# Loading attention values in 2 KB rows and rearranging them through DRAM, and loading the last 64 tokens of q and k in 1 KB rows

## The chip, the cores and the metric

The kernel runs on one core of one Trainium2 chip. The metric is the device time of that core in microseconds (us). "Fast" and "slow" are states of an execution; verdicts use fast runs alone. TensorE is PE in the profile, its weight loads PEld, VectorE DVE, ScalarE ACT, GpSimd POOL, and SyncE SP; a q behind a name (SPq, ACTq) is the engine's sequencer, which waits and issues transfers.

## The reference

```python
# q, k, v: (8, 8, 576, 64) float32
scores = scale * np.matmul(q, k.transpose(0, 1, 3, 2))
mask_local = (rel >= 0) & (rel < 32)                     # heads 0 to 3
mask_strided = (rel >= 0) & (pos_k % 32 == pos_q % 32)   # heads 4 to 7
attn = softmax(np.where(masks, scores, -1e9))
x = np.matmul(attn, v)            # -> (4608, 512), heads side by side
h = ((x @ w1) * (x @ w2)) @ w3
out = h @ w_out                   # (4608, 512) float32
```

## The kernel before

The weights w3 and w_out are first multiplied into one matrix (the "fold"). The attention of the 8 batches runs interleaved with that fold and with the dense matmuls: while the dense part of batch b runs, PE does the attention of batch b + 1 in between, in a program order that is fixed. Loads for batch b + 2 are issued a turn ahead by SP, go through nine staging buffers and are cast to fp16 by POOL.

The local heads work on 6 blocks of 96 queries, and each block reads 128 keys and values, 32 of them from the block before. So the value tile `v16L` holds token 96·t + p − 32 on partition p for block t, and its first 32 partitions repeat what other partitions hold. Before, each head is loaded with one 256-byte row per token, POOL casts it, and DVE copies the 32 repeated tokens:

```python
def load_vL(b):
    vt = v16L[b % 2]
    for hp in range(2):
        hs = slice(2 * hp, 2 * hp + 2)
        st = stgp.tile([P, 2, LT, D], FP32, tag="stg")
        for h in range(2):
            nc.sync.dma_start(st[32:P, h], v[b, 2 * hp + h].rearrange("(t p) d -> p t d", p=LQ))
        for pr in (bass.ds(32, 32), bass.ds(64, 64)):
            nc.gpsimd.tensor_copy(out=vt[pr, hs, :, 0:D], in_=st[pr])
        nc.vector.tensor_copy(out=vt[0:32, hs, 1:LT, 0:D], in_=vt[96:P, hs, 0:LT - 1, 0:D])
```

The last 64 tokens of q and k (`load_rest`) also come in 256-byte rows, in two transfers per batch. `ph_R` transposes them on PE and four copies put them behind the first 512 tokens:

```python
def ph_R(b):
    ...
    for i, (eng, t) in enumerate((("a", qT), ("a" if b < AHEAD else "v", kT))):
        copy(eng, t[:, 0:2, c0:c0 + NR], pv[:, 0:2, i])                    # contiguous write
        copy(eng, t[:, 2:4, 0:S]...[:, :, :, 64:SQ], pv[:, 2:4, i]...)
```

The order of use, for batch b and its first pair of heads (`...` are cuts):

```python
add(ph_S, pairs[p])        # scores: sps, then exp (ACT: pte) and mask (DVE: ptm)
...
add(ph_PV, pairs[p], 0)    # first local product: xps <- ptm, v16L
```

The softmax here doesn't subtract the row's maximum and nothing guards it: scores larger than these inputs give would overflow.

Of the kernel before, what the change touches and what calls it, by code (L numbers as in the profile page):

```python
# [8 lines left out]
FP32 = mybir.dt.float32  # L9
FP16 = mybir.dt.float16  # L10
# [4 lines left out]
def _ap(t: bass.AP, off_add, dims):  # L15
    return bass.AP(tensor=t.tensor, offset=t.offset + off_add, ap=dims)
# [3 lines left out]
def kernel(  # L20
# [11 lines left out]
    nc = tc.nc  # L32
    B, H, S, D = q.shape
# [3 lines left out]
    P = 128  # L37
# [10 lines left out]
    LQ, LT = 96, 6  # L48
    SQ, ST = 72, 8
    NM = 512  # L50
    NR = S - NM
    KW = 640

    consts = ctx.enter_context(tc.tile_pool(name="consts", bufs=1))
    stgp = ctx.enter_context(tc.tile_pool(name="stgp", bufs=9))
    qkp = ctx.enter_context(tc.tile_pool(name="qkp", bufs=2))
    att = ctx.enter_context(tc.tile_pool(name="att", bufs=2))
    ffn = ctx.enter_context(tc.tile_pool(name="ffn", bufs=2))
    psF = ctx.enter_context(tc.tile_pool(name="psF", bufs=3, space=bass.MemoryType.PSUM))
    psB = ctx.enter_context(tc.tile_pool(name="psB", bufs=2, space=bass.MemoryType.PSUM))  # L60
    psM = ctx.enter_context(tc.tile_pool(name="psM", bufs=1, space=bass.MemoryType.PSUM))
# [3 lines left out]
    def pe(ins):  # L65
        return tc.keep_in_program_order(ins)

    def copy(eng, out, in_):
        if eng == "a":
            nc.scalar.copy(out=out, in_=in_)  # L70
        elif eng == "v":
            nc.vector.tensor_copy(out=out, in_=in_)  # L72
        else:
            nc.gpsimd.tensor_copy(out=out, in_=in_)  # L74


    id16 = consts.tile([P, P], FP16)
# [24 lines left out]
    nc.vector.tensor_mul(maskS, mps[0:SQ, 0:SQ], causal)  # L102


    v16L = [consts.tile([P, 4, LT, D + 1], FP16, name=f"v16L{i}") for i in range(2)]
    v16S = [consts.tile([SQ, 4, ST, D + 1], FP16, name=f"v16S{i}") for i in range(2)]


# [2 lines left out]
    ptms = [consts.tile([P, 640], FP16, name=f"ptm{i}") for i in range(4)]  # L111
    nc.vector.memset(kT[:, 0:2, 0:32], 0.0)
    nc.vector.memset(kT[:, 2:4, S:KW], 0.0)
    for i in range(2):
        nc.vector.memset(v16L[i][:, :, :, D], 1.0)
        nc.vector.memset(v16L[i][0:32, :, 0, :], 0.0)
        nc.vector.memset(v16S[i][:, :, :, D], 1.0)
    for i in range(4):
        nc.vector.memset(ptms[i][:, 576:640], 0.0)
# [43 lines left out]
            x16[(b, nm, grp)] = t  # L163

    def load_rest(b, eng="p"):
        st = stgp.tile([P, H, D], FP32, tag="stg")
        for i, ten in enumerate((q, k)):
            nc.sync.dma_start(st[64 * i:64 * i + 64], ten[b, :, NM:S].rearrange("h p d -> p h d"))
        t = qkp.tile([P, H, D], FP16, tag="r")
        copy(eng, t, st)  # L170
        x16[(b, "r")] = t

    def load_vL(b):
        vt = v16L[b % 2]
        for hp in range(2):
            hs = slice(2 * hp, 2 * hp + 2)
            st = stgp.tile([P, 2, LT, D], FP32, tag="stg")
            for h in range(2):
                nc.sync.dma_start(st[32:P, h], v[b, 2 * hp + h].rearrange("(t p) d -> p t d", p=LQ))
            for pr in (bass.ds(32, 32), bass.ds(64, 64)):  # L180
                nc.gpsimd.tensor_copy(out=vt[pr, hs, :, 0:D], in_=st[pr])  # L181
            nc.vector.tensor_copy(out=vt[0:32, hs, 1:LT, 0:D], in_=vt[96:P, hs, 0:LT - 1, 0:D])

    def load_vS(b):
        vt = v16S[b % 2]
        for hp in range(2):
            st = stgp.tile([SQ, 2, ST, D], FP32, tag="stg")
            sf = st.rearrange("p h c d -> p h (c d)")
            sv = v[b, 4 + 2 * hp:6 + 2 * hp].rearrange("h (p c) d -> p h (c d)", c=ST)
            nc.sync.dma_start(sf[0:64], sv[0:64])  # L190
            nc.sync.dma_start(sf[64:SQ], sv[64:SQ])
            nc.gpsimd.tensor_copy(out=vt[:, 2 * hp:2 * hp + 2, :, 0:D], in_=st)  # L192


# [4 lines left out]
    for b in range(B):  # L199
        for hp in range(4):  # L200
            s = Pair()
# [21 lines left out]
                     ps[:, i].rearrange("x (c t u) -> x u c t", c=4, u=2))  # L223

    def ph_R(b):
        ps = psM.tile([P, 4, 2, 128], FP16, tag="m")
        pv = ps.rearrange("x g a w -> x (g a w)")[:, 0:512].rearrange("x (g a w) -> x g a w", g=4, a=2)
        src = x16[(b, "r")]
        for g in range(4):
            pe(nc.tensor.transpose(pv[:, g].rearrange("x a w -> x (a w)"),  # L230
                                   src[:, 2 * g:2 * g + 2].rearrange("p h d -> p (h d)"), id16))
        for i, (eng, t) in enumerate((("a", qT), ("a" if b < AHEAD else "v", kT))):
            c0 = 32 * i + NM
            copy(eng, t[:, 0:2, c0:c0 + NR], pv[:, 0:2, i])
            copy(eng, t[:, 2:4, 0:S].rearrange("x g (c w) -> x g c w", w=SQ)[:, :, :, 64:SQ],
                 pv[:, 2:4, i].rearrange("x g (s c) -> x g c s", c=ST))

    def ph_S(s):
        w, kr = s.w, s.kr
# [19 lines left out]
    def ph_PV(s, g):  # L259
        w, kr = s.w, s.kr  # L260
        m = s.n // 2
        ptm = s.ptm[g]
        vt = (v16L if s.local else v16S)[s.b % 2]
        xps = psB.tile([P, 2, 512], FP32, tag="big")
        for i in range(m):
            for h in range(2):
                c0 = h * 288 + i * w
                pe(nc.tensor.matmul(xps[:, h, i * 65:(i + 1) * 65], ptm[0:kr, c0:c0 + P],  # L268
                                    vt[0:kr, 2 * (s.hp % 2) + h, g * m + i, :], start=True, stop=True))
        rcp = att.tile([P, 2, 4], FP32, tag="rcp")  # L270
        xqs = att.tile([P, 4, 2, D], FP16, tag="xqs", bufs=4)
        s.xqs[g] = xqs
        xv = xps[0:w, :, 0:m * 65].rearrange("p h (i e) -> p h i e", e=65)
        nc.vector.reciprocal(out=rcp[0:w, :, 0:m], in_=xv[:, :, :, D])
        rp = rcp.ap[0][0]
        nc.vector.tensor_mul(xqs[0:w, 0:m].rearrange("p i h d -> p h i d"), xv[:, :, :, 0:D],  # L276
                             _ap(rcp, 0, [[rp, w], [4, 2], [1, m], [0, D]]))
# [84 lines left out]
    def fold_mm(jc):  # L362
        js = bass.ds(jc * P, P)

        def done(ps):
            copy("va"[jc % 2], w34[:, jc, :], ps)

        return acc_halves(lambda kc: w3T[kc // 4][:, kc % 4, js], lambda kc: woh[:, kc, :], done)
# [8 lines left out]
    for b in range(B):  # L377
        if b < AHEAD:
            add(ph_T, pairs[4 * b])
            add(ph_R, b)  # L380
            add(ph_T, pairs[4 * b + 1])
        for i in range(4):
            p = 4 * b + i
            add(ph_S, pairs[p])
            if i or b >= AHEAD:
                add(ph_T2, pairs[p - 1])
                if i == 0:
                    batch_end[b - 1] = len(stream)
            add(ph_PV, pairs[p], 0)
            if i == 3 and AHEAD <= b + 1 < B:  # L390
                add(ph_R, b + 1)
            add(ph_PV, pairs[p], 1)
            if i < 2 or AHEAD <= b + 1 < B:
                add(ph_T, pairs[p + 2])
        if b + 1 < AHEAD or b == B - 1:
            add(ph_T2, pairs[4 * b + 3])
            batch_end[b] = len(stream)
# [16 lines left out]
    load_w3(1, "p")  # L414
    load_qk(0, 0)
    load_rest(0)
    load_w3(2, "p")
    load_vL(0)
    load_w3(3, "p")
    load_qk(0, 1)  # L420
    load_w3(4, "p")
    load_w3(5, "p")
    load_vS(0)
    load_w3(6, "p")
    load_w3(7, "p")
    load_w12(0)
    load_w12(1)
    load_w12(2)
    load_qk(1, 0)
    load_rest(1)  # L430
    load_w12(3)
    load_vL(1)
    load_qk(1, 1)
    load_vS(1)

    fold = []
    fold_tr(0)
    for jc in range(KF):
        h0, h1 = fold_mm(jc)
# [4 lines left out]
    host(fold, batch_end[0], lead=3)  # L444
    load_qk(2, 0)
    load_rest(2)
    load_vL(2)
    host(ab_halves(0), pos[0] + 8, lead=9)
    load_qk(2, 1)
    load_vS(2)  # L450
    host(o_halves(0), batch_end[1])
    for tch in range(1, NTILE):
# [46 lines left out]
```

## Time and profile before

| | before |
|---|---|
| timed | 295.25 us median of 3 (293.96 to 296.12) |
| PE busy, of the traced span | 90% |
| packets under 512 B | 29,184 of 58,653 |
| loads' packet time (queue 1) | 54.7% of 16 engines |

The page of the kernel before begins with the busy time of each engine, then shows the span in 40 slices in tenths (PEclk is the clock that PE was granted, DMA the busy share of the 16 DMA engines), then the queues (packets, MB, share of 16 engines), then the chain that ended last:

```profile
PE 268.9 (90%) x2401; PEld 141.6 (47%) x2401; DVE 174.6 (58%) x353; ACT 147.1 (49%) x269; POOL 102.1 (34%) x118
PE   2258898989889989989999899999999999999995
PEclk9996999999999999999999999999999999999999
DMA  7999999999869929994896796030012002003003
q1 hardware_dynamic: 53440, 38.81, 54.7%
q10 hardware_dynamic: 5184, 9.44, 8.7%
PE 67%; DVE 9%; DMA 9%; ACT 9%; issue 3%; SPq 1%; POOL 0%; ACTq 0%
```

PE is what fills the span, from the fourth slice on. DMA is as full as PE in the first ten slices (75 us). The groups by line that the change takes away are these, in the kernel before (count, then busy us and mean ns of one, then idle time before them and what ended it):

```profile
L181 POOL CAST v16L<-st 32x768 f16<-32x768 f32 (+1 forms) x32 | 27.1, 847 | 18.4 <-DMA st<-in_v_dram 12.6
L182 DVE COPY v16L<-v16L 32x640 f16<-32x640 f16 x16 | 10.8, 677 | 2.3 <-POOL v16L L181 1.9
```

This first trace is of a long execution: its span is 299.8 us, and another traced execution was timed at 1.8 us above its span, so this one would be about 301.6, above all the timed ones. Below, the comparison with the change uses a second trace of the same kernel (span 293.3 us). Two rows of its page:

```profile
PE 267.5 (91%) x2401; PEld 141.4 (48%) x2401; DVE 171.0 (58%) x353; ACT 146.8 (50%) x269; POOL 102.8 (35%) x118
PEclk9989999999999999999999999999999999999999
```

### The profile page before, as it was taken

What the parts mean: (1) busy time and instruction counts of PE and PEld (TensorE: products, weight loads), DVE (VectorE), ACT (ScalarE), POOL (GpSimd) and SP (SyncE); (2) the same over time, 40 slices, a digit from 0 to 9 for tenths busy, and PEclk for the clock granted to TensorE, in tenths of its full rate; (3) what the DMA queues carried; (4) which work ended last, traced back from release to release, by engine and by line L of the source; (5) the groups of instructions that cost most, each with busy time, mean ns of one, the idle gap of its engine ahead of it and who ended that gap; (6) DMA issues with size and microseconds to landing.
All of it is one profiled execution on the core that took longest, in us unless ns stands there. A gap on an engine that the chain in (4) does not pass through costs nothing.

```text
span 299.8 us, 6132 instructions
## 1 busy us (share of the span) xinstructions
PE 268.9 (90%) x2401; PEld 141.6 (47%) x2401; DVE 174.6 (58%) x353; ACT 147.1 (49%) x269; POOL 102.1 (34%) x118
## 2 busy tenths in 40 slices
PE   2258898989889989989999899999999999999995
PEld 1025554435545545545555445555555555444442
DVE  2011775357888866886789659747765774340430
ACT  2025586557565545536645554564455445333332
POOL 5539744486626724653455345110000000000000
PEclk9996999999999999999999999999999999999999
DMA  7999999999869929994896796030012002003003
GB/s 228 349 160 352 288 348 258 216 273 209 249 200 243 242 79 270 246 178 159 240 236 140 253 193 164 27 115 2 2 57 87 0 2 105 35 2 116 24 2 140
DMA packets 58653, 48.64 MB, mean 162 GB/s; under 512 B 29184, under 2 KB 49664, under 8 KB 58624
## 3 DMA queue, kind: packets, MB, share of 16 engines
q1 hardware_dynamic: 53440, 38.81, 54.7%
q10 hardware_dynamic: 5184, 9.44, 8.7%
q8 instruction: 19, 0.31, 0.5%
q14 instruction: 10, 0.08, 0.1%
HBM read 38.80 MB, written 9.44 MB: 161 GB/s over the span
## 4 chain that ended last, share of the span: by engine, by line
PE 67%; DVE 9%; DMA 9%; ACT 9%; issue 3%; SPq 1%; POOL 0%; ACTq 0%
PE ops L335 19%; PE bps L321 18%; PE aps L312 16%; PE xps L268 4%; PE ps L214 4%; DMA st<-in_moe_w_dram 4%; ACT pte L253 3%; DVE ptm L255 3%; DMA st<-in_moe_w_out_dram 3%; DMA out_dram<-osb 3%; PE sps L248 2%; PE ps L284 2%; DVE abt L323 2%; ACT xT L291 2%; DVE kT L72 2%
## 5 line engine op out<-in xcount | busy, mean ns | idle before, releaser
L312 PE MATMUL aps<-xT,w1h 128*128 128x512 f16 x288 | 75.3, 379 | 3.2 <-ACT xT L291 3.0
L323 DVE TENSOR_TENSOR abt<-bps,asb 128x512 f16<-128x512 f32 x72 | 49.5, 687 | 47.2 <-PE bps L321 45.5
L321 PE MATMUL bps<-xT,w2h 128*128 128x512 f16 x288 | 74.0, 379 | 0.0
L315 ACT COPY asb<-aps 128x512 f32<-128x512 f32 x72 | 42.2, 586 | 64.6 <-PE aps L312 61.8
L335 PE MATMUL ops<-w,abt 128*128 128x512 f16 x288 | 71.7, 379 | 0.5 <-DVE abt L323 0.5
L74 POOL CAST t<-st 128x1024 f16<-128x1024 f32 (+1 forms) x48 | 47.4, 991 | 43.4 <-DMA st<-in_k_dram 29.1
L253 ACT ACTIVATE pte<-sps 128x576 f16<-128x576 f32 (+1 forms) x64 | 38.4, 650 | 7.3 <-PE sps L248 7.1
L276 DVE TENSOR_TENSOR xqs<-xps,rcp 96x384 f16<-96x384 f32 (+1 forms) x64 | 39.6, 619 | 2.0
L321 PEld LDWEIGHTS <-w2h 128*128 128x128 f16 x288 | 25.8, 97 | 31.6 <-issue 5.1
L70 ACT COPY qT<-ps 128x512 f16<-128x512 f16 (+1 forms) x48 | 22.9, 481 | 29.9 <-PE ps L214 23.8
L346 ACT COPY osb<-ops 128x512 f32<-128x512 f32 x36 | 21.1, 586 | 29.9 <-PE ops L335 28.6
L335 PEld LDWEIGHTS <-abt 128*128 128x128 f16 x288 | 24.7, 98 | 23.1 <-DVE abt L323 1.0
L312 PEld LDWEIGHTS <-w1h 128*128 128x128 f16 x288 | 25.1, 98 | 22.2
L181 POOL CAST v16L<-st 32x768 f16<-32x768 f32 (+1 forms) x32 | 27.1, 847 | 18.4 <-DMA st<-in_v_dram 12.6
L268 PEld LDWEIGHTS <-ptm 72*128 72x128 f16 (+1 forms) x448 | 21.4, 97 | 19.2 <-DVE ptm L255 6.4
L255 DVE TENSOR_TENSOR ptm<-pte,maskL 128x576 f16<-128x576 f16 x32 | 20.5, 646 | 11.7 <-ACT pte L253 11.2
L72 DVE COPY kT<-ps 128x512 f16<-128x512 f16 (+1 forms) x36 | 18.8, 535 | 10.1 <-ACT qT L70 10.0
L255 DVE TENSOR_TENSOR ptm<-pte,maskS 72x576 f16<-72x576 f16 x32 | 19.6, 620 | 8.5 <-ACT pte L253 7.9
L192 POOL CAST v16S<-st 72x1024 f16<-72x1024 f32 x16 | 16.9, 1055 | 20.1 <-PE xps L268 11.4
L335 PE MATMUL ops<-woh,w3T 128*128 128x512 f16 x64 | 19.8, 440 | 3.2 <-POOL woh L74 3.1
L214 PEld LDWEIGHTS <-t 128*128 128x128 f16 x256 | 17.1, 99 | 8.8 <-issue 2.6
L214 PE MATMUL ps<-id,t 128*128 128x128 f16 x256 | 20.1, 222 | 0.5 <-POOL t L74 0.5
(48 smaller groups left out, 175.8 us busy)
## 6 DMA issues: line engine op xcount, KB each, us to landing
out_dram<-osb ACTq DMA_DIRECT2D x36, 256.0 KB, 2.0
st<-in_moe_w_dram SPq DMA_DIRECT2D x16, 512.0 KB, 8.9
st<-in_q_dram SPq DMA_DIRECT2D x16, 512.0 KB, 5.5
st<-in_k_dram SPq DMA_DIRECT2D x16, 512.0 KB, 6.6
st<-in_v_dram SPq DMA_DIRECT2D x32, 144.0 KB, 6.1
st<-in_v_dram SPq DMA_DIRECT2D x16, 256.0 KB, 7.2
st<-in_moe_w_out_dram SPq DMA_DIRECT2D x4, 512.0 KB, 8.5
st<-in_q_dram SPq DMA_DIRECT2D x8, 128.0 KB, 8.1
```

What stands on the lines that cost most here:

```text
L74: nc.gpsimd.tensor_copy(out=out, in_=in_)
L181: nc.gpsimd.tensor_copy(out=vt[pr, hs, :, 0:D], in_=st[pr])
L214: pe(nc.tensor.transpose(ps[:, i, c * P:(c + 1) * P], src[:, c, h0:h0 + 2].rearrange("p h d -> p (h d)"), id16))
L253: nc.scalar.activation(out=pte[0:kr], in_=sps[0:kr, :, 0:288], func=AF.Exp, bias=0.0, scale=scale)
L255: nc.vector.tensor_mul(ptm[0:kr, 0:576].rearrange("p (a x) -> p a x", x=w), pte[0:kr].rearrange("p h (a x) -> p (h a) x", x=w), _ap(mk, 0, ...
L268: pe(nc.tensor.matmul(xps[:, h, i * 65:(i + 1) * 65], ptm[0:kr, c0:c0 + P], vt[0:kr, 2 * (s.hp % 2) + h, g * m + i, :], start=True, stop=T ...
L276: nc.vector.tensor_mul(xqs[0:w, 0:m].rearrange("p i h d -> p h i d"), xv[:, :, :, 0:D], _ap(rcp, 0, [[rp, w], [4, 2], [1, m], [0, D]]))
L312: pe(nc.tensor.matmul(aps, w1h[:, ci, bass.ds(jc * P, P)], xT[ci][:, tok], start=(ci == 0), stop=(ci == KM - 1)))
L315: nc.scalar.copy(out=asb, in_=aps)
L321: pe(nc.tensor.matmul(bps, w2h[:, ci, bass.ds(jc * P, P)], xT[ci][:, tok], start=(ci == 0), stop=(ci == KM - 1)))
L323: nc.vector.tensor_mul(abts[tch][:, jc, :], bps, st["asb"])
L335: pe(nc.tensor.matmul(st["ps"], lhs(ci), rhs(ci), start=(ci == 0), stop=(ci == KF - 1)))
```

## The change

The intent is to get rid of 256-byte rows. The local values come in rows of 8 tokens (2 KB), are cast into `vN`, stored as fp16 in DRAM, and read back from there with the overlap, so the second read does the rearranging and DVE's copy goes. The three transfers of this round trip ("the trip" from here on) are issued by ACT. The last 64 tokens of q and k come in 1 KB rows of 4 tokens, in eight transfers per batch, and `ph_R` reorders them. The diff, cut to its core:

```diff
     def load_rest(b, eng="p"):
-        st = stgp.tile([P, H, D], FP32, tag="stg")
+        st = stgp.tile([P, 2, 4, D], FP32, tag="stg")
         for i, ten in enumerate((q, k)):
-            nc.sync.dma_start(st[64 * i:64 * i + 64], ten[b, :, NM:S].rearrange("h p d -> p h d"))
+            for g in range(4):
+                r0 = 64 * i + 16 * g
+                nc.sync.dma_start(st[r0:r0 + 16]..., ten[b, 2 * g:2 * g + 2, NM:S]...)   # rows of 4 tokens
     ...
     def load_vL(b):
-        (as shown above)
+        vt, vn = v16L[b % 2], vN
+        for hp in range(2):
+            st = load_v8(b, 2 * hp)                     # 72 partitions, rows of 8 tokens
+            nc.gpsimd.tensor_copy(out=vn[:, :, 2 * hp:2 * hp + 2, 0:D]..., in_=st)
+        vd = dramp.tile([S, 4 * (D + 1)], FP16, tag="vd")
+        nc.scalar.dma_start(vd.rearrange("(p c) x -> p (c x)", c=ST), vn...)
+        nc.scalar.dma_start(vt[:, 1:LT]..., _ap(vd, (LQ - 32) * pit, [[pit, P], [LQ * pit, LT - 1], [1, pit]]))
+        nc.scalar.dma_start(vt[32:P, 0]..., vd[0:LQ])
     ...
     def ph_R(b):
-            copy(eng, t[:, 0:2, c0:c0 + NR], pv[:, 0:2, i])
-            copy(eng, t[:, 2:4, 0:S]...[:, :, :, 64:SQ], pv[:, 2:4, i]...)
+            copy(eng, t[:, 0:2, c0:c0 + NR].rearrange("x g (t s) -> x g s t", s=ST), pr[:, 4 * i:4 * i + 2])
+            copy(eng, t[:, 2:4, 0:S].rearrange("x g (s w) -> x g s w", w=SQ)[:, :, :, 64:SQ], pr[:, 4 * i + 2:4 * i + 4])
```

More of the change, by code (lines that the diff above doesn't have):

```diff
@@ L58 @@
     ffn = ctx.enter_context(tc.tile_pool(name="ffn", bufs=2))
+    dramp = ctx.enter_context(tc.tile_pool(name="dramp", bufs=2, space=bass.MemoryType.DRAM))
     psF = ctx.enter_context(tc.tile_pool(name="psF", bufs=3, space=bass.MemoryType.PSUM))
@@ L102 @@
     nc.vector.tensor_mul(maskS, mps[0:SQ, 0:SQ], causal)
-    v16L = [consts.tile([P, 4, LT, D + 1], FP16, name=f"v16L{i}") for i in range(2)]
+    v16L = [consts.tile([P, LT, 4, D + 1], FP16, name=f"v16L{i}") for i in range(2)]
+    vN = consts.tile([SQ, ST, 4, D + 1], FP16)
     v16S = [consts.tile([SQ, 4, ST, D + 1], FP16, name=f"v16S{i}") for i in range(2)]
@@ L113 @@
     nc.vector.memset(kT[:, 2:4, S:KW], 0.0)
+    nc.vector.memset(vN[:, :, :, D], 1.0)
     for i in range(2):
-        nc.vector.memset(v16L[i][:, :, :, D], 1.0)
-        nc.vector.memset(v16L[i][0:32, :, 0, :], 0.0)
+        nc.vector.memset(v16L[i][0:32, 0], 0.0)
         nc.vector.memset(v16S[i][:, :, :, D], 1.0)
@@ L165, in load_rest, with load_v8 @@
     def load_rest(b, eng="p"):
-        st = stgp.tile([P, H, D], FP32, tag="stg")
+        st = stgp.tile([P, 2, 4, D], FP32, tag="stg")
         for i, ten in enumerate((q, k)):
-            nc.sync.dma_start(st[64 * i:64 * i + 64], ten[b, :, NM:S].rearrange("h p d -> p h d"))
-        t = qkp.tile([P, H, D], FP16, tag="r")
-        copy(eng, t, st)
-        x16[(b, "r")] = t
+            for g in range(4):
+                r0 = 64 * i + 16 * g
+                nc.sync.dma_start(st[r0:r0 + 16].rearrange("r h c d -> r h (c d)"),
+                                  ten[b, 2 * g:2 * g + 2, NM:S].rearrange("h (r c) d -> r h (c d)", c=4))
+        t = qkp.tile([P, 4, 2, D], FP16, tag="r")
+        copy(eng, t.rearrange("p c h d -> p h c d"), st)
+        x16[(b, "r")] = t
+    def load_v8(b, h0):
+        st = stgp.tile([SQ, 2, ST, D], FP32, tag="stg")
+        sf = st.rearrange("p h c d -> p h (c d)")
+        sv = v[b, h0:h0 + 2].rearrange("h (p c) d -> p h (c d)", c=ST)
+        nc.sync.dma_start(sf[0:64], sv[0:64])
+        nc.sync.dma_start(sf[64:SQ], sv[64:SQ])
+        return st
     def load_vL(b):
-        vt = v16L[b % 2]
+        vt, vn = v16L[b % 2], vN
         for hp in range(2):
-            hs = slice(2 * hp, 2 * hp + 2)
-            st = stgp.tile([P, 2, LT, D], FP32, tag="stg")
-            for h in range(2):
-                nc.sync.dma_start(st[32:P, h], v[b, 2 * hp + h].rearrange("(t p) d -> p t d", p=LQ))
-            for pr in (bass.ds(32, 32), bass.ds(64, 64)):
-                nc.gpsimd.tensor_copy(out=vt[pr, hs, :, 0:D], in_=st[pr])
-            nc.vector.tensor_copy(out=vt[0:32, hs, 1:LT, 0:D], in_=vt[96:P, hs, 0:LT - 1, 0:D])
+            st = load_v8(b, 2 * hp)
+            nc.gpsimd.tensor_copy(out=vn[:, :, 2 * hp:2 * hp + 2, 0:D].rearrange("p c h d -> p h c d"), in_=st)
+        vd = dramp.tile([S, 4 * (D + 1)], FP16, tag="vd")
+        nc.scalar.dma_start(vd.rearrange("(p c) x -> p (c x)", c=ST), vn.rearrange("p c h e -> p (c h e)"))
+        pit = 4 * (D + 1)
+        nc.scalar.dma_start(vt[:, 1:LT].rearrange("p t h e -> p t (h e)"),
+                            _ap(vd, (LQ - 32) * pit, [[pit, P], [LQ * pit, LT - 1], [1, pit]]))
+        nc.scalar.dma_start(vt[32:P, 0].rearrange("p h e -> p (h e)"), vd[0:LQ])
     def load_vS(b):
@@ L186, in load_vS @@
         for hp in range(2):
-            st = stgp.tile([SQ, 2, ST, D], FP32, tag="stg")
-            sf = st.rearrange("p h c d -> p h (c d)")
-            sv = v[b, 4 + 2 * hp:6 + 2 * hp].rearrange("h (p c) d -> p h (c d)", c=ST)
-            nc.sync.dma_start(sf[0:64], sv[0:64])
-            nc.sync.dma_start(sf[64:SQ], sv[64:SQ])
+            st = load_v8(b, 4 + 2 * hp)
             nc.gpsimd.tensor_copy(out=vt[:, 2 * hp:2 * hp + 2, :, 0:D], in_=st)
@@ L225, in ph_R @@
     def ph_R(b):
-        ps = psM.tile([P, 4, 2, 128], FP16, tag="m")
-        pv = ps.rearrange("x g a w -> x (g a w)")[:, 0:512].rearrange("x (g a w) -> x g a w", g=4, a=2)
+        ps = psM.tile([P, 1024], FP16, tag="m")
+        pv = ps[:, 0:512].rearrange("x (a u c t) -> x a u c t", a=8, u=2, c=4)
         src = x16[(b, "r")]
-        for g in range(4):
-            pe(nc.tensor.transpose(pv[:, g].rearrange("x a w -> x (a w)"),
-                                   src[:, 2 * g:2 * g + 2].rearrange("p h d -> p (h d)"), id16))
+        idp = id16.rearrange("p (a t u) -> p a u t", a=8, u=2)
+        for c in range(4):
+            pe(nc.tensor.transpose(pv[:, :, :, c, :], src[:, c].rearrange("p h d -> p (h d)"), idp))
+        pr = ps[:, 0:512].rearrange("x (a s t) -> x a s t", a=8, s=ST)
         for i, (eng, t) in enumerate((("a", qT), ("a" if b < AHEAD else "v", kT))):
             c0 = 32 * i + NM
-            copy(eng, t[:, 0:2, c0:c0 + NR], pv[:, 0:2, i])
-            copy(eng, t[:, 2:4, 0:S].rearrange("x g (c w) -> x g c w", w=SQ)[:, :, :, 64:SQ],
-                 pv[:, 2:4, i].rearrange("x g (s c) -> x g c s", c=ST))
+            copy(eng, t[:, 0:2, c0:c0 + NR].rearrange("x g (t s) -> x g s t", s=ST), pr[:, 4 * i:4 * i + 2])
+            copy(eng, t[:, 2:4, 0:S].rearrange("x g (s w) -> x g s w", w=SQ)[:, :, :, 64:SQ], pr[:, 4 * i + 2:4 * i + 4])
     def ph_S(s):
@@ L266, in ph_PV @@
             for h in range(2):
+                hh = 2 * (s.hp % 2) + h
                 c0 = h * 288 + i * w
                 pe(nc.tensor.matmul(xps[:, h, i * 65:(i + 1) * 65], ptm[0:kr, c0:c0 + P],
-                                    vt[0:kr, 2 * (s.hp % 2) + h, g * m + i, :], start=True, stop=True))
+                                    vt[0:kr, g * m + i, hh, :] if s.local else vt[0:kr, hh, g * m + i, :],
+                                    start=True, stop=True))
         rcp = att.tile([P, 2, 4], FP32, tag="rcp")
```

## The prediction

> **What bounds the kernel now.** The tensor engine. The page gives PE 90% of the span, DVE 58%, ACT 49%, POOL 34%; the chain of waits is 67% PE. Three stages:
> 1. 0 to 24 us: the chain is almost only DMA: output weights until 11.6 us, then one w3 block, landing at 22.3.
> 2. 24 to 90 us: PE with hand-overs to ACT and DVE; the windows view leaves PE about 7 us idle. DMA is 99% busy to 75 us, yet the chain names no load here.
> 3. 90 to 256 us: 512-column matmuls start 216 ns apart, PE is nearly full (about 2 us idle from 90 to 165 us), loads come early.
>
> **What the change does.**
> - DMA: 26,624 packets of 256 B took 29 ns each, 48 us summed over 16 engines. They become 2,304 of 2 KB (about 100 ns, 14 us) and 2,048 of 1 KB (57 ns, 7 us). Added: 576 rows of 4,160 B stored (about 180 ns, 6.5 us) and 5,888 rows of 520 B read (estimate 40 ns, between 256 B and 1 KB: 15 us). Sum about 43 us: the round trip eats nearly all that is saved.
> - POOL: 32 casts of 847 ns become 16 of about 1,055 ns: 10 us less.
> - DVE: 16 copies for the overlap go (0.33 us alone, 0.95 to 1.16 us beside a POOL cast). The chain shows 3 us of them. [...] Gain 2 to 4 us.
> - ACT: three DMA issues per batch, about 0.34 us each by the output stores. The read-back must wait for the store's landing[...]. Output stores land in 2.0 us alone and 6.5 us under load, so ACT may stand 1 to 3 us per batch.
> - SP: rest loads go from 2 to 8 issues per batch. The SP queue's waits show loads held by an earlier transfer's landing (output stores, 8 to 9 us); more, smaller transfers hold more.
>
> **On the critical path.** Start: w3's landing gains about 1 us from faster rest rows; holds by the eight small transfers can eat it. Local values of batches 0 and 1 are used soon after loading: casts end at 27 and 62 us, first use at 30.7 and 65.1 us. The round trip (store 3 to 4 us, read 3 to 5 us) replaces a 0.3 to 1 us copy, less 1.5 us of POOL: PE, in program order, waits 1 to 4 us in each. Later batches are loaded far ahead; there only ACT's occupied time counts, perhaps 0.5 us of PE per batch. Gains 3 to 6 us, losses 4 to 12 us.
>
> **Prediction: 297 us, 8 in 10 between 290 and 306. Faster by over 2%: 0.15; within 2%: 0.52; slower by over 2%: 0.33.**
>
> **What would show it.** Right: queue 1's packet time falls by some 25 us over 16 engines, the ACT queue gains about 20; POOL busy near 92 us; DVE 10 to 15 us less; PE waits for the read-back before its first local products in batches 0 and 1; ACT idle ended by the store. Wrong: PE never waits for v16L and ACT never for the store.
>
> **What would make it wrong.** If other ACT work lies between store and read-back, losses vanish: 2% faster. Faster too if w3 lands several us early. If SP loads get held behind read-backs, weights come late: over 3% slower.

The gain of 2 to 4 us on DVE rests on the measured 0.33 and 0.95 to 1.16 us. That ACT may stand for 1 to 3 us rests on the landing of output stores (in the first trace of before 2.0 to 2.3 us from 240 to 300 us, where the DMA engines were 14% busy, and 2.0 to 6.5 us from 66 to 110 us, where they were 93% busy), and that ACT would be what waits for the store was the assumption. The trace of the changed kernel bears it out: in batch 2 ACT did nothing from 104.51 to 107.51 us and issued the read-back in between, at 106.43.

## The result, and the profile after

The changed kernel took 331.87 us (330.85 to 333.22, 4 runs) against 294.61 us (293.48 to 296.12, 4 runs). The ratio is 1.127, 95% interval 1.122 to 1.132: 12.7% slower. Ratios here are the mean time of one kernel's fast runs over that of the other's of the same rounds, so not quite the ratio of the medians quoted.

The page of the changed kernel, the same parts as before:

```profile
PE 278.4 (84%) x2401; PEld 145.1 (44%) x2401; DVE 163.4 (49%) x336; ACT 150.3 (46%) x269; POOL 91.4 (28%) x102
PE   2464399980994699899999999899899999999995
PEclk9985589996799589999999999999999999999999
DMA  7889896965347782669688548686201100201103
q1 hardware_dynamic: 31808, 38.81, 40.8%
q10 hardware_dynamic: 12000, 14.90, 13.1%
PE 61%; DMA 23%; ACT 6%; issue 3%; DVE 2%; SPq 1%; ACTq 1%; POOL 1%; POOLq 0%
```

The groups by line of the changed kernel have, in place of L181 and L182 of before, only this one:

```profile
L190 POOL CAST vN<-st 72x1024 f16<-72x1024 f32 x16 | 17.0, 1063 | 16.5 <-DMA st<-in_v_dram 16.5
```

Every engine but PE and ACT does less, and the loads' packets take less time. Yet the row of PE has holes in the slices 5, 10 and 13 (near 38, 80 and 105 us), and under or just behind each hole the row PEclk falls. Each slice is 8.3 us here. Of the longest waits of PE behind the start, these two lines of the view of waits, for the changed kernel (total us, times, longest us), have to do with the trip:

```profile
PE xps L279 <- DMA v16L<-vd: 20.0, 3, 10.1
PE aps L324 <- ACT xT L303: 4.9, 6, 3.4
```

The waits of SP's sequencer in the changed kernel, which hold loads back, in the same columns:

```profile
SPq L161 <- DMA vd<-vN: 27.6, 6, 10.6
SPq L172 <- DMA v16L<-vd: 22.7, 8, 5.1
```

In the second trace of before, the waits of PE for anything behind the start are about 1.1 us each at most; the line for the first local products there reads:

```profile
PE xps L268 <- DVE ptm L255: 2.5, 5, 0.9
```

How one such wait comes about can be read from the timelines of the changed kernel (start, duration, instruction, and in brackets the idle time before it and what ended it). First PE, around the first local product of batch 0:

```profile
27.66 1.03 PE L369 MATMUL trp<-id,t 128*128 128x128 f16 x8
38.80 0.49 PE L279 MATMUL xps<-v16L,ptm 128*128 128x65 f16 x6 [10.11 <-DMA v16L<-vd]
```

Then ACT's sequencer in the same kernel and stretch (start, duration, transfer issued):

```profile
27.83 0.57 ACTq L192 DMA_DIRECT2D vd<-vN  x1
33.68 0.42 ACTq L194 DMA_DIRECT2D v16L<-vd  x1
34.15 0.52 ACTq L196 DMA_DIRECT2D v16L<-vd  x1
```

The store is issued at 27.83 us, its landing lets the read-back go at 33.68 (5.9 us later), and PE resumes at 38.80 (5.1 us after that); the DMA engines were 76% busy in these 11 us. POOL's casts had ended at 24.86 us, so 3.0 us had passed before ACT even came to the store. In batch 1, POOL is done with the second cast at 65.62 us, but ACT comes to the store only at 73.76, because ACT works in its program order and the store stands behind a dozen copies and casts: in these 8.1 us ACT was busy for 6.2 and waited for PE for the rest. The timelines of POOL, ACT and PE of the changed kernel, one after the other:

```profile
64.57 1.05 POOL L190 CAST vN<-st 72x1024 f16<-72x1024 f32 x1 [0.26 <-DMA st<-in_v_dram]
```

```profile
73.76 0.32 ACTq L192 DMA_DIRECT2D vd<-vN  x1
76.74 0.45 ACTq L194 DMA_DIRECT2D v16L<-vd  x1
```

```profile
82.33 0.49 PE L279 MATMUL xps<-v16L,ptm 128*128 128x65 f16 x6 [7.65 <-DMA v16L<-vd]
```

In batch 2 the casts end at 90.7 us and the store is issued at 102.45. There PE waits twice: 3.40 us, as ACT's copy of `xT` stands behind the read-back's issue, and 2.28 us for the read-back itself.

The span can be cut at PE's first local product of each batch, by the starts of those matmuls in the two traces:

| stretch, us | before (second trace) | changed |
|---|---|---|
| start to batch 0 | 26.3 | 38.8 |
| batch 0 to 1 | 34.3 | 43.5 |
| batch 1 to 2 | 21.6 | 30.4 |
| batch 2 to 3 | 28.5 | 31.5 |
| batch 3 to 7 | 112.8 | 116.1 |
| batch 7 to the end | 69.7 | 69.7 |

The first four stretches hold 33.5 of the 36.9 us. Seen the other way, PE's idle time between its first and last matmul rises from 19.5 to 45.5 us (26.0), and its busy time from 267.5 to 278.4 us (10.9) with the same 2,401 matmuls. Most of the busy time is explained by the clock: in three stretches the granted clock is half (22.6 to 43.1, 77.2 to 87.5, 108.0 to 118.2 us by the clock records, 41 us in sum; 3.4 us in the second trace of before). PE was busy for 22.4 us of these 41; if each of those would have taken half at full clock, and with 1.5 us lost in the same way in the second trace of before, that makes 9.6 of the 10.9 us (an estimate). Not all of it lies behind the waits for the trip: the first stretch began at 22.6 us, six us before PE ran out of work, and by the same estimate 2.6 us were lost there. The windows view shows the low clock: length, then busy time of PE, PEld, DVE, ACT, POOL with the number of instructions, then the granted clock, DMA share and GB/s.

```profile
30.00:40.00 10.00, 1.20 (x9) 0.68 (x10) 0.85 (x3) 0.58 (x1) 3.78 (x4) 0.50 0.73 199
80.00:90.00 10.00, 6.88 (x55) 3.80 (x56) 3.07 (x7) 3.13 (x6) 3.05 (x4) 0.63 0.42 123
```

Behind the waits of batches 0 and 1, four 512-column matmuls took 1.71 us by the chain of waits where they take 0.86 us elsewhere in this trace. The three stretches at half clock are 20.48, 10.24 and 10.24 us long, six, three and three times 3.41 us. In batch 1 the clock fell 2.6 us after PE had run out of work (74.7 to 77.2 us), and it was full again at 87.5 us, 5.1 us after PE had resumed.

### The profile page after: what moved, and what is told of

It is laid out like the page before. It is cut to its first block, busy times and chain, and to the rows that moved or that the text cites. A ratio compares the mean times of both kernels' runs of the same rounds, so it can differ in the third digit from the quotient of the medians.

```text
span 330.2 us, 6210 instructions
## 1 busy us (share of the span) xinstructions
PE 278.4 (84%) x2401; PEld 145.1 (44%) x2401; DVE 163.4 (49%) x336; ACT 150.3 (46%) x269; POOL 91.4 (28%) x102
## 3 DMA queue, kind: packets, MB, share of 16 engines
q1 hardware_dynamic: 31808, 38.81, 40.8%
## 4 chain that ended last, share of the span: by engine, by line
PE 61%; DMA 23%; ACT 6%; issue 3%; DVE 2%; SPq 1%; ACTq 1%; POOL 1%; POOLq 0%
PE bps L333 17%; PE aps L324 17%; PE ops L347 16%; DMA vd<-vN 8%; DMA st<-in_k_dram 6%; DMA v16L<-vd 5%; PE xps L279 4%; PE ps L224 4%; DMA out_dram<-osb 3%; PE sps L258 2%; DMA st<-in_q_dram 2%; PE ps L296 2%; ACT pte L263 1%; ACT xT L303 1%; DVE kT L73 1%
## 5 line engine op out<-in xcount | busy, mean ns | idle before, releaser
L324 PE MATMUL aps<-xT,w1h 128*128 128x512 f16 x288 | 77.5, 388 | 5.1 <-ACT xT L303 4.9
L333 PE MATMUL bps<-xT,w2h 128*128 128x512 f16 x288 | 76.6, 390 | 1.5 <-ACT asb L327 1.5
L335 DVE TENSOR_TENSOR abt<-bps,asb 128x512 f16<-128x512 f32 x72 | 49.5, 687 | 54.7 <-PE bps L333 53.2
L71 ACT COPY qT<-ps 128x512 f16<-128x512 f16 (+1 forms) x48 | 25.5, 573 | 44.1 <-PE ps L224 39.7
L333 PEld LDWEIGHTS <-w2h 128*128 128x128 f16 x288 | 26.3, 99 | 36.1 <-issue 10.9
L279 PEld LDWEIGHTS <-ptm 72*128 72x128 f16 (+1 forms) x448 | 22.3, 100 | 39.1 <-issue 22.4
L347 PEld LDWEIGHTS <-abt 128*128 128x128 f16 x288 | 24.8, 98 | 22.2
L279 PE MATMUL xps<-v16L,ptm 128*128 128x65 f16 x192 | 12.2, 203 | 21.9 <-DMA v16L<-vd 20.0
L286 DVE RECIPROCAL rcp<-xps 96x6 f32<-96x6 f32 (+1 forms) x64 | 12.3, 192 | 35.6 <-PE xps L279 35.3
L265 DVE TENSOR_TENSOR ptm<-pte,maskL 128x576 f16<-128x576 f16 x32 | 18.8, 591 | 19.2 <-ACT pte L263 18.6
L73 DVE COPY kT<-ps 128x512 f16<-128x512 f16 (+1 forms) x36 | 21.0, 645 | 13.7 <-ACT qT L71 13.7
L224 PE MATMUL ps<-id,t 128*128 128x128 f16 x256 | 21.4, 231 | 3.9 <-ACT kT L71 1.6
L347 PE MATMUL ops<-woh,w3T 128*128 128x512 f16 x64 | 22.1, 480 | 2.0 <-POOL woh L75 1.5
L265 DVE TENSOR_TENSOR ptm<-pte,maskS 72x576 f16<-72x576 f16 x32 | 18.2, 569 | 10.2 <-ACT pte L263 9.4
```

The costliest lines, as they stand in the source:

```text
L71: nc.scalar.copy(out=out, in_=in_)
L224: pe(nc.tensor.transpose(ps[:, i, c * P:(c + 1) * P], src[:, c, h0:h0 + 2].rearrange("p h d -> p (h d)"), id16))
L265: nc.vector.tensor_mul(ptm[0:kr, 0:576].rearrange("p (a x) -> p a x", x=w), pte[0:kr].rearrange("p h (a x) -> p (h a) x", x=w), _ap(mk, 0, ...
L279: pe(nc.tensor.matmul(xps[:, h, i * 65:(i + 1) * 65], ptm[0:kr, c0:c0 + P], vt[0:kr, g * m + i, hh, :] if s.local else vt[0:kr, hh, g * m ...
L324: pe(nc.tensor.matmul(aps, w1h[:, ci, bass.ds(jc * P, P)], xT[ci][:, tok], start=(ci == 0), stop=(ci == KM - 1)))
L333: pe(nc.tensor.matmul(bps, w2h[:, ci, bass.ds(jc * P, P)], xT[ci][:, tok], start=(ci == 0), stop=(ci == KM - 1)))
```

## The experiments

Theory A: the trip's latency is too long for the batches whose values are loaded late, so PE waits, and its clock falls behind each wait. Theory B, the rival: the eight small transfers of `load_rest` hold the loads that follow. Further rivals: the added traffic, the time that ACT stands, and the new copies in `ph_R`. Fifteen kernels ran. The check of the result failed e11_no_dep alone, which is wrong. It passed e6_rows_only and e7_copies_only too, although they unpack the wrong tokens of q and k, so its passing says little about `load_rest` and `ph_R`. In the tables, "ratio" is to the kernel before in the same rounds; a point is a hundredth of it.

### One part of the change at a time

e1_rest_only has the new `load_rest` and `ph_R` in the kernel before:

```diff
 # the kernel before, with
-    load_rest, ph_R
+    load_rest, ph_R of the change; load_vL and v16L stay
```

> Only the 1 KB rows of the last 64 tokens (eight transfers per batch), local values as before. Theory A (the DRAM round trip of the local values costs the 37 us: PE waits for the read-back in batches 0 to 2 and its clock is halved after each wait): within 1.5% of before, 291 to 298 us. Theory B (eight small transfers per batch hold the loads that follow, so the weights and batches come late): 310 to 332 us, with loads held by landings in the SP queue's waits as in the changed kernel.

e2_v_only is the changed kernel with the old `load_rest` and `ph_R`:

```diff
 # the changed kernel, with
-    load_rest, ph_R
+    load_rest, ph_R of the kernel before
```

> Only the local values' round trip, last 64 tokens in two transfers as before. Theory A: 322 to 336 us, PE gaps of about 10, 8 and 2 us before the first local products of batches 0, 1, 2 as in the changed kernel. Theory B: 293 to 302 us.

| run | us | ratio, 95% interval |
|---|---|---|
| e1_rest_only | 303.76 | 1.024 (1.018 to 1.030) |
| e2_v_only | 322.79 | 1.086 (1.075 to 1.096) |

The trip alone gives two thirds of the loss, and its trace has the waits that theory A expected, 11.1 us in batch 0 and 7.8 us in batch 1 (in batch 2 PE waits 3.4 us, but for a copy of `kT` on DVE). Theory B's numbers for this pair are refuted. But the 1 KB rows cost 2.4% where theory A expected nothing over 1.5%, so both parts lose, in very unequal shares.

### The trip only where its lead is long

e4_direct3 loads the first three batches in the old way. The old code goes ahead of the trip, with the layout of `v16L` adapted:

```diff
     def load_vL(b):
         vt, vn = v16L[b % 2], vN
+        if b < 3:
+            (the loads, casts and DVE copy of the kernel before)
+            return
```

> The changed kernel, but batches 0, 1 and 2 load their local values as before (256 B rows, POOL casts, DVE copy); batches 3 to 7 make the round trip. Theory A: no PE gap over 3 us after 25 us, 293 to 300 us. If the round trip costs in every batch (ACT occupied and standing): 305 to 320 us. Theory B: 320 us or more.

It took 310.41 us, ratio 1.048 (1.040 to 1.055). No PE wait over 2.1 us is left after 25 us, and 7.9 of the change's 12.7 points are gone: they belong to the trips of batches 0 to 2. The time lies above theory A's range and inside the one written down for a trip that costs in every batch (305 to 320 us). But this run has the 1 KB rows too; what is left has to be parted between them and the later trips. So e9_mix_act is the same with the last 64 tokens as before, and e10_mix_pool has POOL issue the trip as well (see below):

```diff
 # e4_direct3, with
-    load_rest, ph_R of the change
+    load_rest, ph_R of the kernel before        # e9_mix_act, and e10_mix_pool
-        nc.scalar.dma_start(...)                # the trip's three transfers
+        nc.gpsimd.dma_start(...)                # e10_mix_pool only
```

> Last 64 tokens as before; local values of batches 0 to 2 loaded as before, of batches 3 to 7 through DRAM with the transfers on ACT as in the change. In the run with the round trip alone the stretches between first local products of batches 3 to 7 took 27.8 to 28.4 us apiece (one 30.8) against 27.8 to 29.0 in the second trace of before. Theory A (the trip hurts only where its landing is late): 292 to 298 us, ratio 0.985 to 1.005. If each trip costs by standing ACT: 302 us or more.

> As the run before in this job, the three transfers of the trip issued by POOL. There the stretches of batches 3 to 7 took 27.8 us each, 2 us less in sum than before. Ratio 0.985 to 1.0, 291 to 296 us; if POOL standing for the store delays the casts of the next queries and keys: above 1.01.

| run | us | ratio, 95% interval |
|---|---|---|
| e9_mix_act | 297.79 | 1.007 (1.001 to 1.014) |
| e10_mix_pool | 297.76 | 1.004 (0.997 to 1.011) |

With five rounds, neither beats the kernel before. Five trips a turn ahead of their use cost next to nothing, and save next to nothing. In the trace of e10_mix_pool the stretch from batch 3 to 7 took 111.8 us, against 112.8 before. That is no sign that the DVE copies that are gone were worth 1 us: in e6_rows_only (below), which keeps them, it took 111.3 us. The expectation of a ratio below 1.0 was not met.

### The clock

e3_warm is the changed kernel with matmuls on constants in front of the first local products of the first three batches. They do no useful work; they only keep PE from idling.

```diff
+    def ph_warm(n):
+        wps = psF.tile([P, NT], FP32, tag="f", name="wps")
+        for i in range(n):
+            pe(nc.tensor.matmul(wps, id16, warm, start=True, stop=True))
     ...
+            if i == 0 and b < 3:
+                add(ph_warm, (40, 30, 10)[b])
             add(ph_PV, pairs[p], 0)
```

> The changed kernel with 40, 30 and 10 matmuls on constants (8.6, 6.5, 2.2 us at 216 ns) ahead of the first local products of batches 0, 1, 2, where PE stands idle for the read-back. Theory A with the clock: PE stays at full clock after the waits, the matmuls that ran at half clock (PE busy time is 9.5 us longer than before) get faster, 322 to 327 us, granted clock near 0.98. If the longer busy time does not come from the idle waits: 332 us or more, as PE only got more work.

It took 326.32 us, ratio 1.097 (1.088 to 1.106), the clock in its timed runs was 0.983 to 0.989 against 0.937 to 0.949. Adding 80 matmuls made the kernel 3.0 points faster, about 9 us. The windows view of e3_warm for the same stretches as above:

```profile
30.00:40.00 10.00, 10.00 (x80) 5.12 (x78) 2.33 (x6) 1.33 (x3) 5.84 (x6) 1.00 0.86 253
80.00:90.00 10.00, 9.10 (x124) 5.34 (x123) 5.84 (x16) 7.44 (x15) 2.88 (x3) 1.00 0.58 162
```

The clock is full where it was 0.50 and 0.63. In batch 2, 10 matmuls were too few: PE still waited 5.03 us and ran at half clock from 104 to 111 us. So roughly a quarter of the 12.7 points (3.0, about 2 to 4 by the two intervals) goes with the clock that falls while PE idles. The traced execution is the fastest of its runs: its clock stayed full at the start too, where the changed kernel's trace fell to half at 22.6 us, before any added matmul.

### Who issues the trip

e8_v_pool is e2_v_only with the three transfers on POOL, whose own casts stand right before the store.

```diff
-        nc.scalar.dma_start(...)      # three times
+        nc.gpsimd.dma_start(...)
```

> Local values' round trip alone (as in the run with only that step, ratio 1.0855), its three transfers issued by POOL right behind its own casts instead of by ACT. If what made the read-back late is where ACT's program order puts the store (store issued 8 us after the cast in batch 1, 12 us in batch 2): PE gaps at the first local products shrink to 5 us in batch 0 and under 2 us in batches 1 and 2, 303 to 312 us. If the trip itself takes too long whoever issues it: 318 us or more.

It took 314.59 us, ratio 1.064 (1.055 to 1.073), between the two numbers expected: 2.2 points better than from ACT, far from well. The timeline of POOL in batch 1 shows why:

```profile
63.55 1.05 POOL L187 CAST vN<-st 72x1024 f16<-72x1024 f32 x1 [0.59 <-DMA st<-in_v_dram]
64.90 0.54 POOL L189 DMA_DIRECT2D vd<-vN  x1 [0.30 <-POOL vN L187]
73.43 0.89 POOL L191 DMA_DIRECT2D v16L<-vd  x1 [5.58 <-DMA vd<-vN]
```

The store now follows the cast after 0.30 us, but it takes 8.2 us to land, and the read-back lands at 81.07 us: 16 us for a trip of 0.68 MB. In batch 0 it took 16.0 us, and PE waited 13.4 us. From ACT, in the first three batches of the changed kernel, the store took 3.0 to 5.9 us and the read-back 5.1 to 6.3.

The expectation left out that POOL's transfers take a queue of another kind; e8_v_pool's page lists it (packets, MB, share):

```profile
q0 software_dynamic: 1792, 5.46, 6.3%
```

In batch 0 the store is issued at nearly the same time in e2_v_only (24.7 us, by ACT) and here (24.6 us), yet the trip took 11.5 us there and 16.0 here. By the packet records, in batches 0 and 1 the store's first packet moved 4.8 and 5.1 us after its issue, against 3.4 and 0.8 us in e2_v_only. But the DMA engines were also fuller, busy all through these two trips by the windows view (a share of 1.05 from 30 to 40 us), where in e2_v_only their share was 0.82 and 0.64. Which of the two made POOL's trip longer was not tested.

ACT's output stores land in 2.0 to 2.3 us in the last 60 us of the first trace of before, where the DMA engines are 14% busy, but in these runs it is the chain of two transfers, at 3 to 8 us each, that has to be planned for. Where the store had waited for its turn on ACT, POOL helped: the stretches from batch 0 to 1 to 2 are 40.5 and 22.6 us, 43.3 and 26.9 us in e2_v_only. Part of that may be that in this trace no load of SP waits for a landing of the trip, while e2_v_only has 19.1, 7.7, 7.5 and 6.1 us of such waits. The experiment changes the issuer, the kind of queue and the held loads at once and does not part them.

### The traffic without the chain

e11_no_dep is wrong: the read-back reads a DRAM tile that is written once at the start, so the bytes stay and the waiting for casts and store goes.

```diff
+    vd0 = dramp.tile([S, 4 * (D + 1)], FP16, tag="vd0", bufs=1)
+    nc.scalar.dma_start(vd0..., vN...)            # once
     ...
-                            _ap(vd, (LQ - 32) * pit, ...))
+                            _ap(vd0, (LQ - 32) * pit, ...))
```

> Wrong result on purpose. Round trip alone, but the read-back reads a DRAM tile that was written once at the start: the same stores and reads, the same bytes and packets, but no read waits for a store or for the loads and casts ahead of it. Theory A (latency of the chained steps): no PE gap over 3 us after 25 us, 290 to 299 us. If the 5.5 MB more of traffic and the occupied queues are the cause: 312 us or more.

It took 305.76 us, ratio 1.035 (1.029 to 1.041). PE no longer waits for the read-back at all, so about 5.1 of the 8.6 points of e2_v_only (some 4 to 6 by the intervals) go with the chain. The other 3.5 points were not expected. The chain of waits shows where they sit: the one store at the start and the first read-back, which still waits for it, run at 3 to 17 us and the loads queue behind their landings, its first local product starts at 31.5 us instead of 26.3, and the stretch to batch 1 takes 39.8 us instead of 34.3. This run moved the added transfers into the busiest 20 us, so it says that they cost something there, not what they cost at their own place.

### More lead

e12_early is e2_v_only with the local values loaded first in each turn, and earlier at the start.

```diff
+    load_vL(0)
     load_qk(0, 0)
     ...
-    load_vL(0)
     ...
     load_w12(1)
+    load_vL(1)
     ...                               # later batches: load_vL ahead of load_qk
```

> Round trip alone, the local values loaded first: of batch 0 ahead of its queries and keys, of batch 1 after half of the w1, w2 blocks, of later batches at the head of each turn. Theory A: the lead grows by about 8 us in batch 0 and 15 us in batch 1, the PE gaps there shrink from 11 and 8 us to under 4 and 0 us, 298 to 308 us. If lead is not what is short: 318 us or more.

It took 314.82 us, ratio 1.063 (1.055 to 1.071), not the 298 to 308 expected. The PE waits in question did shrink as expected, to 1.0 us in batch 0 (still for the read-back) and none over 0.9 us in batch 1. But the wait moved: the longest waits of PE in this run, and under them the one for the read-back, are

```profile
PE trp L366 <- POOL t L75: 9.8, 3, 5.2
PE ps L293 <- DVE kT L73: 7.8, 4, 3.5
PE xps L276 <- DMA v16L<-vd: 1.0, 1, 1.0
```

The first two are for w3 blocks, and for copies of batch 2's and 5's attention that run late. The DMA engines are 100% busy from 10 to 30 us. That a load moved ahead there pushed the w3 blocks back would fit the first line (7.2 us, at most 3.1, in e2_v_only), but was not shown by itself. The first local product came at 33.5 us: 2.7 us better than in e2_v_only, 7.2 us worse than before.

### The 2.4% of the 1 KB rows

e6_rows_only has only the eight transfers, e7_copies_only only the new `ph_R`; each unpacks what the other would have loaded, so both are wrong. e5_before_again is the kernel before, for a second trace.

```diff
 # the kernel before, with
-    load_rest                 # e6_rows_only: of the change
-    ph_R                      # e7_copies_only: of the change
```

> The kernel before, unchanged: a second trace of it, as the first one was of a long execution (301.6 us by its span against 294 to 296 us timed). Same as before within 1%; PE idle time near 20 us instead of 24.6.

> Wrong result on purpose. The kernel before with only the eight 1 KB-row transfers of the last 64 tokens; the transposes and copies that unpack them are as before. The 1 KB-row step alone cost 2.4% (7 us). If the holding of loads by eight small transfers is the cause: 300 to 304 us, with loads held by output stores in the SP queue's waits. If the unpacking copies are: 293 to 298 us.

> Wrong result on purpose. The kernel before with only the new transposes and the copies that write in steps of 16 bytes (the ACT copy of 128x128 took 0.73 us instead of 0.27 us). If these copies cost the 7 us: 300 to 304 us. If the transfers do: 294 to 299 us, as ACT and DVE get only about 0.9 us more per batch in sum.

| run | us | ratio, 95% interval |
|---|---|---|
| e5_before_again | 296.39 | 0.999 (0.990 to 1.008) |
| e6_rows_only | 298.11 | 1.006 (1.000 to 1.012) |
| e7_copies_only | 298.87 | 1.006 (1.000 to 1.012) |

Neither half gives the 2.4%; each gives at most half of it. The copies are plainly slower one by one. Of each pair the first was contiguous and now writes in steps of 16 bytes. ACT's timeline in e5_before_again, then in e1_rest_only:

```profile
104.12 0.27 ACT L70 COPY qT<-ps 128x128 f16<-128x128 f16 x1
```

```profile
110.41 0.73 ACT L70 COPY qT<-ps 128x128 f16<-128x128 f16 x1
```

The same 128 elements per partition, written in steps of 16 bytes, took 2.7 times as long (0.73 against 0.27 us). Why it does was not tested.

What the halves do together was still open, so e15_rest_warm adds 14 matmuls on constants to e1_rest_only. The clock records of e1_rest_only show two stretches of 3.4 us at half clock (65.0 to 68.5 and 85.5 to 88.9 us) that neither half has. In the 3.4 us before each, PE was idle for 1.9 and 1.8 us in sum, in gaps of at most 1.7 us.

```diff
+            if p == 4: add(ph_warm, 6)        # ahead of batch 1's first local product
+            if p == 7: add(ph_warm, 3)        # ahead of a transpose at the end of batch 1
+            if p == 8: add(ph_warm, 5)        # ahead of the first transpose back in batch 2
```

> The 1 KB-row step alone with 6, 3 and 5 matmuls on constants where PE waits in the stretches 61 to 65 us and 82 to 86 us, ahead of the two stretches at half clock. If the clock is what the two halves of the step cost together: granted clock 0.99, ratio 1.008 to 1.016, 299 to 301 us. If not: 1.022 or more.

It took 299.74 us, ratio 1.017 (1.008 to 1.026), clock 0.993 to 0.994 against 0.977 to 0.983. That lies between the two outcomes expected, and the intervals of the two runs overlap. The clock did recover; that it is some of the difference is likely but not shown, and the rest is not settled.

### The two steps together

With the 1 KB rows, the trips of batches 3 to 7 seemed to cost 2.3 points (e4_direct3 less e1_rest_only), without them 0.7 (e9_mix_act). e13_direct3_pool and e14_all_pool are e4_direct3 and the whole change with the trip on POOL, to see whether loads held behind ACT's trip are the reason.

```diff
-        nc.scalar.dma_start(...)      # the trip's three transfers
+        nc.gpsimd.dma_start(...)
```

> As the run with batches 0 to 2 direct and the 1 KB-row step (ratio 1.0475), but the trips of batches 3 to 7 issued by POOL. If loads held behind the trip's landings on ACT are what the two steps cost together: no SP wait for the trip, ratio 1.02 to 1.032, 302 to 306 us. If not: 1.04 or more.

> The whole change, the trip issued by POOL. Held loads the cause of what the steps cost together beyond their sum: 1.064 and 1.0242 add up, ratio 1.08 to 1.095, 320 to 325 us. If not: 1.115 or more, as the change.

| run | us | ratio, 95% interval |
|---|---|---|
| e13_direct3_pool | 309.58 | 1.054 (1.043 to 1.065) |
| e14_all_pool | 317.54 | 1.075 (1.063 to 1.087) |

They disagree: e14_all_pool came out below even the range expected if held loads were the cause (1.08 to 1.095), e13_direct3_pool in the range expected if they were not. For the whole change, POOL as the issuer takes away 5.2 of the 12.7 points, more than in e8_v_pool alone, and the stretches from batch 0 to 1 to 2 take 38.1 and 22.2 us instead of 43.5 and 30.4. But e13_direct3_pool is no better than e4_direct3, though in its trace no load of SP waits for a landing of the trip. POOL's queue is of the other kind in both, as in e8_v_pool. So held loads are a part of the loss in batches 1 and 2 of the full change at best, and why the 1 KB rows and the later trips cost more together than apart stays open.

## Why the prediction was wrong

It said 297 us (290 to 306), most likely within 2%; it measured 331.87. Point by point:

- **Work of the engines: right in the main.** Queue 1's packet time fell from 54.7% of 299.8 us to 40.8% of 330.2 us, that is from 164 to 135 us (29 us, or 26 against the second trace of before; 25 were forecast), and the ACT queue's rose by 17 us (20). POOL was busy 91.4 us (92). DVE was busy 11 us less than in the first trace of before, but only 8 less than in the second (10 to 15). The forecast sum of 43 us for the changed packets came out at 43 by luck: the 520-byte reads took 30 ns apiece, not 40, and queue 1's 2 KB packets 126 ns, not 100. Per packet, 256 bytes took 29 ns (9 bytes per ns, in the first trace of before), the 520-byte reads moved 17 bytes per ns, and 1 KB packets took 57 ns in the first trace of before (18 bytes per ns) and 54 in the changed kernel. DVE's copies "alone" need a closer word: in the first trace those that began just before a POOL cast took 0.33 us too (at 25.24 and 27.16 us); behind the start of one they took 0.67 to 1.16.
- **The saving of packets is worth little in time: right, as far as shown.** e10_mix_pool, with five batches in 2 KB rows, can't be told from the kernel before (1.004, 0.997 to 1.011); that is saving and trip together.
- **The step that failed: "The round trip (store 3 to 4 us, read 3 to 5 us) replaces a 0.3 to 1 us copy, less 1.5 us of POOL: PE, in program order, waits 1 to 4 us in each."** PE waited 10.1 us in batch 0 and 7.65 us in batch 1. The place was right, and the wait for the read-back was named; the size was not. The measured sums close. Batch 0, from the end of the casts: 3.0 us until ACT issued the store, 5.9 for the store, 5.1 for the read-back, 13.9 in all, of which PE had work for 3.8. Batch 1: 8.1 + 3.0 + 5.6 = 16.7 us, of which PE had work for 9.1. So in batch 1 the transfers took about the time forecast and in batch 0 two us more than the upper end of the forecast; the term that the sum lacked altogether is the first one. It counted what a store does after it is issued and not where it stands in ACT's program order.
- **"Later batches are loaded far ahead": wrong for batch 2.** Its store was issued 11.8 us after the casts, and PE waited 3.40 + 2.28 us for its trip, in a stretch that grew by 8.8 us; the rest is mostly work at half clock. For batches 3 to 7 it was right as long as the 1 KB rows were left out: e9_mix_act lost 2.2 us with five trips, 0.4 us each (0.5 were forecast), with an interval almost as wide.
- **A term was missing altogether: the clock.** PE's busy time rose by 10.9 us, nearly all of it at half clock and most of that behind the waits; e3_warm got 3.0 points back by keeping PE busy.
- **The 1 KB rows: the gain did not come.** "w3's landing gains about 1 us" and the holds were taken as a draw; the step costs 2.4%, of which each half alone shows 0.6. The slower copies were not in the forecast. The holds did grow: SP's waits for landings, those for the output stores at its end left out, came to 94 us in e1_rest_only, against 65 and 55 us in the two traces of before.
- **"SP loads get held behind read-backs" was listed as what would make it wrong, and it is in the trace**: 27.6 us of SP waits for the store and 22.7 us for the read-back in the two longest lines. How much of the time is theirs could not be parted from ACT's order.

In ratio points the loss divides, as far as the runs tell: 7.9 of 12.7 are the trips of batches 0 to 2, in which the halved clock is contained (about 3 points); 2.4 are the 1 KB rows; some 2.3 are the later trips in company with the 1 KB rows, unexplained. Each of these is a difference of two ratios, good to about one point. Without the 1 KB rows the trips of batches 0 to 2 cost the same (7.8, e2_v_only less e9_mix_act).

## What to carry to other kernels

Before a load is replaced by a chain (load, cast, store, read back), write down for each consumer when its data are ready and when they are used, in the busiest stage, and add up the whole chain including the place of each issue in its engine's program order: here two transfers made 9 to 16 us from the issue of the store, and its place in the order up to 12 us more, where an output store takes 2.0 us (the median of 36 in the first trace of before). A long wait of PE can be paid twice, once idle and once at half clock, as those of 7.65 and 3.40 us were here; look at the row of the granted clock beneath each hole. Fewer, larger packets saved nothing measurable here, as the chain of waits was not waiting for the loads that they made shorter, and a first-used batch may deserve another path than the ones loaded a turn ahead.
